# Two more groups' output products by Strassen's seven products, and v of 13 tiles loaded as float by SyncE, in a fused retention and feed-forward kernel on one Trainium2 core

## The chip, the cores and the metric

One core of one Trainium2 chip runs the whole program. Its engines are TensorE (PE; its weight loads are listed as PEld), VectorE (DVE), ScalarE (ACT), GpSimd (POOL) and SyncE (SP), each with its own queue of instructions; they wait for each other by semaphores. The metric is device time in microseconds (us) of one execution. Of the kernel before, three runs gave 205.72, 205.92 and 206.09 us, a median of 205.92 us.

## What is computed

Retention over 4 batches, 8 heads, 768 tokens and 64 columns a head, then a feed-forward network on the 3072 tokens, 512 wide with 2048 hidden columns:

```python
for t in range(S):
    state = gamma[None, :, None, None] * state + np.einsum('bhd,bhe->bhde', k[:, :, t], v[:, :, t])
    y[:, :, t] = scale * np.einsum('bhd,bhde->bhe', q[:, :, t], state)
...
x = np.ascontiguousarray(attn_out.transpose(0, 2, 1, 3)).reshape(B * S, H * D)
...
h = x @ w_in
s = np.sin(alpha * h)
g = h + s * s / (alpha + 1e-09)
return (g @ w_out).astype(np.float32)
```

Inputs and output are float32. The kernel holds operands in bfloat16 and adds up in float32.

## The kernel before, in words

**Tiles, groups, phases.** The 3072 tokens are 24 tiles of 128 (six chunks for each batch). A list P sets their order, and they form ten groups, g = 0 to 9: four tiles, then eight pairs, then four tiles. The recurrence is computed by chunks: for a tile the products of q and k, masked, times v, plus q times the state that the earlier chunks left (`burst` for one tile, `pair` for two). The result is the group's xT, the input of its feed-forward part. Up to the middle of group 1 the order of all work is written out in a list of words; from group 2 on it is set by `phase(g)`.

**A phase.** `phase(g)` computes the hidden layer of group g and, woven into it, the output of group g - 1. For a pair of tiles it has eight slots. A `Slot` takes two of the 16 hidden blocks: 8 matmuls 256 columns wide into a PSUM tile ph (L610), the sine on ScalarE (L613), its square on ScalarE (L618) and, one slot later, h + s²/α on VectorE into gT (`add`, L625). Behind the matmuls of each slot stand those of the output of group g - 1. In some slots `att` puts the attention of a later group in between, and what it leaves to VectorE follows: masks (L404, L407), the state's update (L568, L572) and, in the next two slots, the two halves of xT (`exit0`, `exit1`, L561). `at((g, n), ...)` names such a place by phase and slot; `mixes((g, n), ...)` puts work behind the slot's VectorE work.

**The output in the plain way.** 32 matmuls 512 wide for a pair of tiles (L634, four to a slot), then a copy of each tile from PSUM by VectorE (L644) and its store by SyncE (L647).

**The output by seven products.** For groups in `fast` (before: the pair of group 8 and the two pairs of group 9) the 2x2 blocks of tiles, hidden halves and output columns are multiplied by Strassen's seven products: 56 matmuls 256 wide for a pair (class `Seven`, `mm`, L756). They need sums and differences of gT blocks (`mix_g`, L710, three instructions for two slots' blocks: s, d and x) and of w_out blocks (`mix_w`, L681). The products add up in three PSUM tiles, a, b and c. b is copied to SBUF (`hold`, L765 on ScalarE or L767 on VectorE), and VectorE forms the four output blocks: `cross` (L791, a + b), `rest` (L796, c - b), `main` (L801, a + rest).

**PSUM.** Tag `mm` has four banks, which ph, the plain output and the separate score tiles pb share; `pa` and `two` are tiles of two banks each. The pair's y lies in `two`.

**Loads and turns.** The last 13 tiles of P (`wide`) are read in sets for each batch by `load_seq`: eight transfers for q, k or v, one for each head, issued by GpSimd and converted to bfloat16 on the way (L149). `load_chunk` reads v of earlier tiles (L125). Before a tile's attention its q and k are transposed by a DMA that SyncE issues (`turn`, L297), and its v is multiplied by its decay (`scale_v`, L189) on VectorE or GpSimd. The places of these calls stand at the end of the program, in the tables of `at` and `mixes`.

**Numbers of lines.** All line numbers are those of the kernel before; in the changed kernel L149 is L155, L189 is L197, L297 is L304, L404 and L407 are L411 and L414, L495 is L502, L515 is L522, L561 is L568, L568 is L575, L572 is L579, L610, L613, L618 and L625 are L617, L620, L625 and L632, L644 is L651, L681 is L686, L710 is L717, L756 is L763, L765 is L772, and L791, L796 and L801 are L798, L803 and L808.

Of the kernel before, what the change touches and what calls it, by code (L numbers as in the profile page):

```python
# [38 lines left out]
def kernel(  # L39
# [90 lines left out]

    def load_seq(bt, names="qkv", part=slice(None), between=None):
# [8 lines left out]
        fs = slice(2 * (now[0] - cs[0]), 2 * (now[-1] - cs[0]) + 2)  # L140
        for name, src in (("q", q), ("k", k), ("v", v)):
            if name not in names:
                continue
            for n, (b, m, e) in enumerate(heads):
                if n == 3 and between is not None:
                    scale_v(between, nc.gpsimd)
                r, at = half(b), 2 * m + e
# [1 line left out]
                nc.gpsimd.dma_start(out=o, in_=src[bt, head(b, m, e), now[0] * C:(now[-1] + 1) * C, :].rearrange("(f i) d -> i f d", i=64))  # L149
# [35 lines left out]
    def scale_v(j, eng):  # L185
        t, by = raw["v", j], kg
        if wide(j):
            t, by = t.rearrange("i f p d -> i (f p) d"), kgq
        eng.tensor_mul(t, t, by[:, j % NCH, :, None].to_broadcast([128, H, D]))  # L189

# [473 lines left out]
    w_todo = [(n, i) for n in (4, 3, 1, 7, 6) for i in range(2)]

    def w_homes():
        for _ in range(5):
            yield big.tile([128, 4, NH], BF16, name="w_mix", tag="qkr", bufs=10)
        for pool, tag, n in ((consts, "dec", 2), (big, "qk_seq1", 3)):
            t = pool.tile([128, n, 4, NH], BF16, name="w_mix", tag=tag)  # L670
            for i in range(n):
                yield t[:, i]
    w_home = w_homes()

    def mix_w(eng):

        n, i = w_todo.pop(0)
# [3 lines left out]
        eng.tensor_tensor(w_mix[n, i], w_block(*a, js), w_block(*b, js), op=op)  # L681

# [37 lines left out]
    class Seven:  # L720
# [20 lines left out]
        def right(self, n, j):  # L741
            if n in (5, 2):
                return w_out[:, j + FH * (n == 5), NH * (n == 5):NH * (n == 5) + NH]
            return w_mix[n, j // 4][:, j % 4]

# [303 lines left out]
    load_seq(1, "v")
    load_seq(2, "q")  # L1050
    load_seq(2, "k")
    load_seq(2, "v")
    load_seq(3, "q", slice(0, 2))
    load_seq(3, "k", slice(0, 2))
    for j in P[15:17] + P[18:19]:
        scale_v(j, nc.gpsimd)

# [27 lines left out]
    at((8, 6), B(P[23], None, None, None, None))  # L1085
    for i, spot in ((19, (6, 1)), (20, (6, 5)), (21, (7, 1)), (22, (7, 5)), (23, (8, 0))):
        at(spot, X(P[i]))
    for i, spot in ((19, (6, 2)), (20, (6, 6)), (21, (7, 2)), (22, (7, 6)), (23, (8, 2))):
        at(spot, lambda j=P[i]: scale_v(j, nc.gpsimd))

    def last_loads():
        mix_w(nc.gpsimd)
        nc.gpsimd.tensor_copy(seen, st["qkT", P[17]][:, 0, 0:1])
        load_seq(3, "v")
        mix_w(nc.gpsimd)
        mix_w(nc.gpsimd)
# [50 lines left out]
```

## Time and profile before

| | us |
|---|---|
| median of three runs | 205.92 |
| the profiled execution's own time | 207.02 |
| its span, first to last instruction | 205.2 |
| PE busy | 195.2 |
| DVE busy | 161.5 |
| ACT busy | 151.8 |
| POOL busy | 163.2 |

Times in a profile start at the span's start. In a group's row the busy time and the mean of one instruction in ns stand behind the first bar, the idle time ahead of these instructions and what ended it behind the second. In a timeline the row gives start, busy time, engine, line, operation, and in brackets the idle time ahead of it. The mean granted clock of TensorE was 0.997.

### The profile page before, as it was taken

How to read it: one execution, taken by the hardware profiler on the slowest of the kernel's cores; microseconds unless marked ns; L12 is line 12 of the kernel's file. 1: busy time of each engine (PE TensorE's matmuls, PEld its weight loads, DVE VectorE, ACT ScalarE, POOL GpSimd, SP SyncE). 2: the span in 40 equal slices, each digit the busy share in tenths (PEclk: the TensorE clock that was granted, in tenths of full speed). 3: DMA queues.
4: the chain of work that ended last, by engine and by line, in shares of the span. 5: the costliest groups of instructions: out<-in, count | busy, mean ns of one | idle time of the engine just before them, and what ended most of it. 6: DMA issues, size and time to landing. Idle time of an engine off the chain costs nothing.

```text
span 205.2 us, 6029 instructions
## 1 busy us (share of the span) xinstructions
PE 195.2 (95%) x2426; PEld 131.4 (64%) x2455; DVE 161.5 (79%) x344; ACT 151.8 (74%) x312; POOL 163.2 (80%) x204
## 2 busy tenths in 40 slices
PE   7889999999998999999999999999999999999993
PEld 7444544557765667666666676666766665555983
DVE  5787499877998887887998885995998775577853
ACT  7678888656996877877877959588586869999120
POOL 8998996999999996997399997999193876997000
PEclk9999999999999999999999999999999999999998
DMA  8999999999999999999996796994406101001123
GB/s 133 147 175 192 201 201 176 167 134 106 231 151 188 104 171 194 170 136 150 143 116 117 89 141 117 120 131 104 105 2 107 51 5 51 3 0 51 54 102 102
DMA packets 103580, 24.82 MB, mean 121 GB/s; under 512 B 93392, under 2 KB 101248, under 8 KB 103552
## 3 DMA queue, kind: packets, MB, share of 16 engines
q0 software_dynamic: 80080, 13.38, 92.8%
q1 hardware_dynamic: 23472, 11.06, 26.8%
q8 instruction: 19, 0.31, 0.7%
q14 instruction: 9, 0.07, 0.1%
HBM read 27.30 MB, written 6.29 MB: 164 GB/s over the span
## 4 chain that ended last, share of the span: by engine, by line
PE 83%; DMA 7%; POOL 4%; issue 2%; DVE 2%; ACT 1%; POOLq 0%
PE ph L610 37%; PE po L634 28%; DMA qkT<-qkr 4%; PE a L756 3%; DMA qkr<-in_q_dram 3%; PE ab L756 3%; POOL qkr L125 2%; PE b L756 2%; PE py L373 1%; POOL vr L125 1%; PE c L756 1%; PE pt L291 1%; PE pa L388 1%; PE py L437 1%; POOL w_in L161 1%
## 5 line engine op out<-in xcount | busy, mean ns | idle before, releaser
L625 DVE SCALAR_TENSOR_TENSOR gT<-s,rec_alpha,ph 128x256 bf16<-128x256 f32 (+3 forms) x164 | 79.4, 522 | 25.1 <-ACT s L618 24.6
L610 PE MATMUL ph<-xT,w_in 128*128 128x256 bf16 (+3 forms) x653 | 98.0, 291 | 0.3
L613 ACT ACTIVATE s<-ph,alpha_sb 128x256 f32<-128x256 f32 (+3 forms) x164 | 75.9, 505 | 28.1 <-PE ph L610 26.3
L610 PEld LDWEIGHTS <-w_in 128*128 128x128 bf16 x656 | 63.1, 98 | 29.6 <-DVE s_f L568 0.7
L634 PE MATMUL po<-w_out,gT 128*128 128x512 bf16 x264 | 70.3, 379 | 2.3 <-issue 1.9
L618 ACT ACTIVATE s<-s 128x512 f32<-128x512 f32 (+1 forms) x94 | 58.7, 626 | 2.8
L634 PEld LDWEIGHTS <-gT 128*128 128x128 bf16 x288 | 26.4, 98 | 20.8 <-DVE gT L625 0.5
L710 POOL TENSOR_TENSOR g_mix<-gT 128x512 bf16<-128x512 bf16 (+1 forms) x27 | 25.9, 994 | 7.2 <-DVE gT L625 7.2
L149 POOL DMA_DIRECT2D qk_seq<-in_q_dram x32 | 21.5, 712 | 6.6 <-DMA v_seq<-in_v_dram 6.1
L149 POOL DMA_DIRECT2D qk_seq<-in_k_dram x32 | 21.3, 720 | 1.5 <-DMA qk_seq<-in_q_dram 1.4
L149 POOL DMA_DIRECT2D v_seq<-in_v_dram x24 | 16.8, 743 | 0.0
L681 POOL TENSOR_TENSOR w_mix<-w_out 128x1024 bf16<-128x1024 bf16 x7 | 15.2, 2190 | 0.0
L756 PEld LDWEIGHTS <-g_mix 128*128 128x128 bf16 x128 | 11.9, 98 | 3.6
L644 DVE COPY o_sb<-po 128x512 f32<-128x512 f32 x15 | 10.3, 687 | 2.0 <-PE po L634 1.6
L125 POOL DMA_DIRECT2D vr<-in_v_dram x11 | 10.3, 932 | 1.2 <-DMA w_in<-in_moe_w_in_dram 0.7
L189 POOL TENSOR_TENSOR v_seq<-v_seq,kgq 128x512 bf16<-128x512 bf16 x9 | 9.8, 1097 | 1.4 <-DMA v_seq<-in_v_dram 1.4
L407 DVE TENSOR_TENSOR aTw<-pa,maskq 128x768 bf16<-128x768 f32 x10 | 9.5, 954 | 0.0
L495 DVE TENSOR_TENSOR xT<-py,qg 128x512 bf16<-128x512 f32 x13 | 8.9, 683 | 0.5 <-PE py L453 0.5
L869 PE MATMUL spare<-warm 128*128 128x112 bf16 (+1 forms) x52 | 7.9, 325 | 1.4 <-DVE warm L199 1.2
L391 DVE TENSOR_TENSOR aT<-pa,mask 128x1024 bf16<-128x1024 f32 x7 | 8.5, 1219 | 0.4 <-PE pa L388 0.4
L520 ACT CAST s_q<-s_f 128x256 bf16<-128x256 f32 x13 | 5.1, 393 | 2.7 <-DVE s_f L515 2.7
L165 POOL DMA_DIRECT2D w_out<-in_moe_w_out_dram x8 | 5.8, 727 | 1.2 <-DMA w_in<-in_moe_w_in_dram 0.8
(138 smaller groups left out, 217.7 us busy)
## 6 DMA issues: line engine op xcount, KB each, us to landing
out_dram<-o_sb SPq DMA_DIRECT2D x21, 256.0 KB, 3.9
w_in<-in_moe_w_in_dram POOLq DMA_DIRECT2D x8, 256.0 KB, 8.3
w_out<-in_moe_w_out_dram POOLq DMA_DIRECT2D x8, 256.0 KB, 7.9
vr<-in_v_dram POOLq DMA_DIRECT2D x11, 128.0 KB, 5.3
v_seq<-in_v_dram POOLq DMA_DIRECT2D x16, 80.0 KB, 4.7
qkr<-in_q_dram POOLq DMA_DIRECT2D x7, 128.0 KB, 6.4
qkr<-in_k_dram POOLq DMA_DIRECT2D x7, 128.0 KB, 5.8
qk_seq<-in_q_dram POOLq DMA_DIRECT2D x16, 48.0 KB, 4.4
```

Of the source, the lines that this page charges most:

```text
L125: nc.gpsimd.dma_start(out=t, in_=chunk_of(src, j))
L149: nc.gpsimd.dma_start(out=o, in_=src[bt, head(b, m, e), now[0] * C:(now[-1] + 1) * C, :].rearrange("(f i) d -> i f d", i=64))
L189: eng.tensor_mul(t, t, by[:, j % NCH, :, None].to_broadcast([128, H, D]))
L610: nc.tensor.matmul(self.ph[:, m, :], w_in[:, i, f * 128:(f + 1) * 128], xT[g][:, i, self.lo:self.hi], start=(m == 0 and i == 0), stop=(i = ...
L613: nc.scalar.activation(out=self.s[:, m, :], in_=self.ph[:, m, :], func=ACTF.Sin, scale=alpha_sb[:, f:f + 1])
L618: nc.scalar.activation(out=self.s, in_=self.s, func=ACTF.Square)
L625: nc.vector.scalar_tensor_tensor(gT[self.g][:, f, self.lo:self.hi], self.s[:, m, :], rec_alpha[:, f:f + 1], self.ph[:, m, :], op0=ALU.mult ...
L634: nc.tensor.matmul(po[g, ts], gT[g][:, f, ts * C:(ts + 1) * C], w_out[:, f, :], start=(f == 0), stop=(f == FF - 1))
L644: nc.vector.tensor_copy(o_sb, po[g, ts])
L681: eng.tensor_tensor(w_mix[n, i], w_block(*a, js), w_block(*b, js), op=op)
L710: eng.tensor_tensor(o, i0, i1, op=op)
L756: nc.tensor.matmul(t, self.left(n, j), r, start=k not in self.begun, stop=(j == FH - 1), skip_group_check=True)
```

## The change

1. **Two more groups by seven products.** `fast` goes from (8, 9) to (6, 7, 8, 9), so that the outputs of groups 6 and 7 take seven products each, in phases 7 and 8: five pairs in place of three. `fast_pieces` writes out for each which products stand in which slot, and the PSUM tiles: for group 7 a, b and c in `mm`; for group 6 a in `mm`, b and c one after the other in `two`. `hold` of both goes to ScalarE. `mix_g` for groups 6 and 7 goes to GpSimd, at the places that only group 8 had. `exit1` comes ahead of the slot's `add` in slot 5 of phases 7 to 9.
2. **w_mix** is made early, in phases 2 to 5, in smaller pieces and other homes; two pieces on VectorE, the others on GpSimd.
3. **v of the 13 tiles** comes as float32 by SyncE into a tile vf, which shares its place with gT of groups 0 and 9; `scale_v` reads vf and writes the bfloat16 v. All but P[9]'s of the scales that VectorE had go to GpSimd.
4. **The last q** comes in one set of eight transfers in place of two.
5. **Turns** of P[12], P[17], P[18] and P[19] are issued earlier, and the loads' places move into the phases.
6. The two blocks of a `store_both` go out by one transfer, except in group 8.

The core of the diff:

```diff
-                nc.gpsimd.dma_start(out=o, in_=src[bt, head(b, m, e), now[0] * C:(now[-1] + 1) * C, :].rearrange("(f i) d -> i f d", i=64))
+                o = vf[r, fs, at, :] if name == "v" else tqk[r, fs, "qk".index(name), at, :]
+                (nc.sync if name == "v" else nc.gpsimd).dma_start(out=o, in_=src[bt, head(b, m, e), now[0] * C:(now[-1] + 1) * C, :].rearrange("(f i) d -> i f d", i=64))
...
     def scale_v(j, eng):
         t, by = raw["v", j], kg
+        o = t
         if wide(j):
-            t, by = t.rearrange("i f p d -> i (f p) d"), kgq
-        eng.tensor_mul(t, t, by[:, j % NCH, :, None].to_broadcast([128, H, D]))
+            o, t = (x.rearrange("i f p d -> i (f p) d") for x in (t, raw["vf", j]))
+            by = kgq
+        eng.tensor_mul(o, t, by[:, j % NCH, :, None].to_broadcast([128, H, D]))
...
-    fast = (8, 9)
+    fast = (6, 7, 8, 9)
...
-            if self.g < NG - 1:
+            if self.g == NG - 2:
                 self.store(0, o[:, 0], n)
                 self.store(1, o[:, 1], 1 - n)
                 return
...
+        if g == NG - 3:
+            s = Seven(g, 0, lambda k: psum.tile([128, 2, NH], F32, name=k, tag="mm", bufs=4)[:, slice(0, 2) if k != "c" else 0])
+            parts = [[(4, range(7))], [(4, range(7, FH)), (3, range(6))], [(3, range(6, FH)), (5, range(5))],
+                     [(5, range(5, FH)), (2, range(4))], [(2, range(4, FH)), s.hold], [s.cross, (1, J)], [s.rest, (7, J)],
+                     [(6, J), s.main]]
+            return [s.steps(*p) for p in parts]
+        if g < NG - 3:
+            def between(k):
+                if k == "a":
+                    return psum.tile([128, 2, NH], F32, name=k, tag="mm", bufs=4)
+                return psum.tile([128, 2, 512], F32, name=k, tag="two")[:, 0].rearrange("p (x n) -> p x n", x=2)[:, slice(0, 2) if k == "b" else 0]
+            s = Seven(g, 0, between)
+            parts = [[(4, J)], [(5, J)], [(2, J), s.hold], [(3, J), s.cross], [(7, range(6))], [(7, range(6, FH)), (6, range(4))],
+                     [(6, range(4, FH)), (1, range(3))], [(1, range(3, FH)), s.rest, s.main]]
+            return [s.steps(*p) for p in parts]
...
+            if g - 1 in fast and n == 5:
+                run(more, "exit1")
...
-    for spot in ((7, 0), (7, 2), (7, 6), (7, 7)):
-        mixes(spot, lambda: mix_w(nc.gpsimd))
-    for m in range(0, FH, 2):
-        mixes((8, m + 1), lambda m=m: mix_g(8, m, 2, nc.gpsimd))
...
+    for g in (6, 7, 8):
+        for m in range(0, FH, 2):
+            mixes((g, m + 1), lambda g=g, m=m: mix_g(g, m, 2, nc.gpsimd))
```

What this makes of GpSimd's queue between phases 2 and 4, right behind the k of batch 1 (qk_seq_1194 before, qk_seq_1193 after) and v of P[10] (vr): before, v of batches 1 and 2 stands between the loads of q and k (v_seq_1195 and v_seq_1224; qk_seq_1223 is batch 2's and qk_seq_1249 batch 3's).

```order
L149 DMA qk_seq_1194<-in_k_dram 64x6x64 x8
L125 DMA vr<-in_v_dram 128x8x64
L149 DMA v_seq_1195<-in_v_dram 64x6x64 x8
L149 DMA qk_seq_1223<-in_q_dram 64x10x64 x8
L149 DMA qk_seq_1223<-in_k_dram 64x10x64 x8
L149 DMA v_seq_1224<-in_v_dram 64x10x64 x8
L149 DMA qk_seq_1249<-in_q_dram 64x4x64 x8
L149 DMA qk_seq_1249<-in_k_dram 64x4x64 x8
L189 TENSOR_TENSOR v_seq_1224<-v_seq_1224,kgq 128x512 x3
```

The same place of GpSimd's queue after (qk_seq_1357 is batch 2's, qk_seq_1384 batch 3's; the first scale is that of P[10], the last two are those of P[14] and P[15]).

```order
L125 DMA vr<-in_v_dram 128x8x64
L686 TENSOR_TENSOR w_mix<-w_out 128x512 x2
L197 TENSOR_TENSOR vr<-vr,kg 128x512
L686 TENSOR_TENSOR w_mix<-w_out 128x512 x2
L155 DMA qk_seq_1357<-in_q_dram 64x10x64 x8
L155 DMA qk_seq_1357<-in_k_dram 64x10x64 x2
L197 TENSOR_TENSOR v_seq_1194<-vf,kgq 128x512
L155 DMA qk_seq_1357<-in_k_dram 64x10x64 x6
L197 TENSOR_TENSOR v_seq_1194<-vf,kgq 128x512 x2
L686 TENSOR_TENSOR w_mix<-w_out 128x512 x3
L155 DMA qk_seq_1384<-in_q_dram 64x10x64 x8
L155 DMA qk_seq_1384<-in_k_dram 64x4x64 x8
```

The 16 transfers of v have left this queue; seven small w_mix and four scales, one of them of P[10], stand in it instead.

On VectorE, phase 7 from slot 3 to slot 6, before: the copy of the first output tile, the attention of the pair that follows, and the two halves of xT with an `add` between them.

```order
L644 COPY o_sb<-po 128x512
L625 SCALAR_TENSOR_TENSOR gT<-s,rec_alpha,ph 128x256 x2
L407 TENSOR_TENSOR aTw<-pa,maskq 128x768
L568 TENSOR_TENSOR s_f<-s_f,pa 128x256
L625 SCALAR_TENSOR_TENSOR gT<-s,rec_alpha,ph 128x256 x2
L572 TENSOR_TENSOR s_f<-s_f,pb_3016 128x128
L572 TENSOR_TENSOR s_f<-s_f,pb_3017 128x128
L404 TENSOR_TENSOR aTw<-pb_3016,maskq 128x384
L404 TENSOR_TENSOR aTw<-pb_3017,maskq 128x384
L561 TENSOR_TENSOR xT<-y,qg 128x2x2x128
L625 SCALAR_TENSOR_TENSOR gT<-s,rec_alpha,ph 128x256 x2
L561 TENSOR_TENSOR xT<-y,qg 128x2x2x128
```

The same place on VectorE after: the crossed blocks of group 6 stand where the copy stood, both halves of xT come together, and `rest` and `main` follow two `add`s later.

```order
L798 TENSOR_TENSOR o_sb<-a,b_sb 128x512
L632 SCALAR_TENSOR_TENSOR gT<-s,rec_alpha,ph 128x256 x2
L414 TENSOR_TENSOR aTw<-pa,maskq 128x768
L575 TENSOR_TENSOR s_f<-s_f,pa 128x256
L632 SCALAR_TENSOR_TENSOR gT<-s,rec_alpha,ph 128x256 x2
L579 TENSOR_TENSOR s_f<-s_f,pb_3072 128x128
L579 TENSOR_TENSOR s_f<-s_f,pb_3073 128x128
L411 TENSOR_TENSOR aTw<-pb_3072,maskq 128x384
L411 TENSOR_TENSOR aTw<-pb_3073,maskq 128x384
L568 TENSOR_TENSOR xT<-y,qg 128x2x2x128 x2
L632 SCALAR_TENSOR_TENSOR gT<-s,rec_alpha,ph 128x256 x4
L803 TENSOR_TENSOR t_sb<-c,b_sb 128x512
```

The second half of xT is one `add` earlier in the queue, and the copy of one output tile is replaced by a sum that needs b's copy on ScalarE.

More of the change, by code (lines that the diff above doesn't have):

```diff
@@ L129, in wide, with load_seq @@
         return j >= NCH + 3 and j % NCH > 0
-    def load_seq(bt, names="qkv", part=slice(None), between=None):
+    def load_seq(bt, names="qkv", part=slice(None), between={}, some=slice(None)):
         cs = [c for c in range(NCH) if wide(bt * NCH + c)]
@@ L140, in load_seq @@
         fs = slice(2 * (now[0] - cs[0]), 2 * (now[-1] - cs[0]) + 2)
+        if "v" in names and "vf" not in raw:
+            raw["vf"] = work.tile([128, 16, NP, D], F32, name="vf", tag="gA", bufs=1)
         for name, src in (("q", q), ("k", k), ("v", v)):
@@ L143, in load_seq @@
                 continue
-            for n, (b, m, e) in enumerate(heads):
-                if n == 3 and between is not None:
-                    scale_v(between, nc.gpsimd)
+            if name == "v":
+                vf = raw["vf"][:, 6:16] if bt == 2 else raw["vf"][:, 0:nh]
+                for i, c in enumerate(cs):
+                    raw["vf", bt * NCH + c] = vf[:, 2 * i:2 * i + 2]
+            for n, (b, m, e) in list(enumerate(heads))[some]:
+                if n in between:
+                    between[n]()
                 r, at = half(b), 2 * m + e
-                o = tv[r, fs, at, :] if name == "v" else tqk[r, fs, "qk".index(name), at, :]
-                nc.gpsimd.dma_start(out=o, in_=src[bt, head(b, m, e), now[0] * C:(now[-1] + 1) * C, :].rearrange("(f i) d -> i f d", i=64))
+                o = vf[r, fs, at, :] if name == "v" else tqk[r, fs, "qk".index(name), at, :]
+                (nc.sync if name == "v" else nc.gpsimd).dma_start(out=o, in_=src[bt, head(b, m, e), now[0] * C:(now[-1] + 1) * C, :].rearrange("(f i) d -> i f d", i=64))
         for i, c in enumerate(cs):
@@ L663, with mix_w @@
              6: ((0, 0), (0, 1), ALU.add), 7: ((1, 0), (1, 1), ALU.add)}
[L664 to L677, printed above, removed]
-        a, b, op = W_MIX[n]
-        js = slice(4 * i, 4 * i + 4)
-        w_mix[n, i] = next(w_home)
-        eng.tensor_tensor(w_mix[n, i], w_block(*a, js), w_block(*b, js), op=op)
+    w_todo = {"vr": [(n, j, 2) for n in (7, 6) for j in range(0, FH, 2)] + [(1, 4, 2), (1, 6, 2)],
+              "dec": [(4, 0, 4), (4, 4, 4)], "seq": [(3, 0, 4), (3, 4, 4), (1, 0, 4)]}
+    w_home = {}
+    def mix_w(eng, home):
+        n, i, c = w_todo[home].pop(0)
+        a, b, op = W_MIX[n]
+        if home == "vr":
+            to = big.tile([128, 2, NH], BF16, name="w_mix", tag="vr", bufs=11)
+        else:
+            if home not in w_home:
+                w_home[home] = (consts if home == "dec" else big).tile(
+                    [128, 2 if home == "dec" else 3, 4, NH], BF16, name="w_mix", tag="dec" if home == "dec" else "qk_seq1")
+            to = w_home[home][:, (2 if home == "dec" else 3) - 1 - len(w_todo[home])]
+        eng.tensor_tensor(to, w_block(*a, slice(i, i + c)), w_block(*b, slice(i, i + c)), op=op)
+        for j in range(c):
+            w_mix[n, i + j] = to[:, j]
     def blocks(t, first, *dims):
@@ L743, in right @@
                 return w_out[:, j + FH * (n == 5), NH * (n == 5):NH * (n == 5) + NH]
[L744 removed]
+            return w_mix[n, j]
         def mm(self, n, j, half=None):
@@ L810, in main, with steps @@
                 self.store(1, self.o[:, 1, c], 1, c.start, c.stop)
+        def steps(self, *parts):
+            return [fn for part in parts for fn in ([part] if callable(part) else self.pieces(part))]
         def pieces(self, *parts):
@@ L878, in phase @@
     def phase(g, outs, att, nf=1, on_vector=(), tags={}, early=()):
-        no, done = len(outs), 0
+        plan = outs if outs and isinstance(outs[0], list) else None
+        no, done = 0 if plan else len(outs), 0
         for n in range(FF // nf):
@@ L901, in phase @@
                 rest[0] = fresh
+            for fn in plan[n] if plan else ():
+                fn()
             while done < min(no, no * (n + 1) * nf // FF):
@@ L1044, with scaled @@
         act(word)
-    load_seq(1, "q", between=P[8])
+    def scaled(*js):
+        return lambda: [scale_v(j, nc.gpsimd) for j in js]
+    load_seq(1, "q", between={3: scaled(P[8])})
     load_seq(1, "k")
     load_chunk(P[10], "v")
[L1049 to L1056, printed above, removed]
     where = {}
@@ L1072, in B, with pieces_w @@
         return lambda: burst(old, new, first, beside=beside, second=second)
+    def pieces_w(n, home):
+        return lambda: [mix_w(nc.gpsimd, home) for _ in range(n)]
     for n in range(9, 17):
@@ L1077 @@
         at(where[n], B(P[n - 1], new, first, P[17] if n == 16 else None, e3 if n == 15 else None))
-        at(where[n] if n < 16 else (5, 5), X(P[n + 2]))
+        if n != 10:
+            at({15: (4, 6), 16: (4, 5)}.get(n, where[n]), X(P[n + 2]))
     for i, spot in ((16, (6, 4)), (18, (7, 4)), (20, (8, 1))):
@@ L1091, in last_loads @@
     def last_loads():
[L1092 to L1096, printed above, removed]
+        load_seq(3, "k", slice(2, None))
+        scale_v(P[16], nc.gpsimd)
         scale_v(P[17], nc.gpsimd)
-        load_seq(3, "qk", slice(2, None))
     at((5, 5), last_loads)
-    for i, spot in ((9, (2, 3)), (10, (3, 0)), (11, (3, 3)), (12, (3, 7)), (13, (4, 3)), (14, (4, 6))):
+    for i, spot in ((9, (2, 3)),):
@@ L1102, with loads @@
         at(spot, lambda j=P[i]: scale_v(j, nc.vector))
     at((2, 0), later_mask)
+    def loads():
+        load_seq(1, "v")
+        turn(P[12])
+        pieces_w(2, "vr")()
+        scale_v(P[10], nc.gpsimd)
+        pieces_w(2, "vr")()
+        load_seq(2, "q")
+        load_seq(2, "k", between={2: scaled(P[11])})
+        scale_v(P[12], nc.gpsimd)
+        scale_v(P[13], nc.gpsimd)
+        pieces_w(3, "vr")()
+        load_seq(3, "q")
+        load_seq(3, "k", slice(0, 2))
+    at((2, 2), loads)
@@ L1113 @@
+    for spot in ((4, 2), (4, 3)):
+        mixes(spot, lambda: mix_w(nc.vector, "vr"))
+    for spot, fn in (((3, 6), scaled(P[14], P[15])), ((3, 6), pieces_w(1, "dec")),
+                     ((3, 6), pieces_w(1, "dec")), ((4, 5), pieces_w(3, "seq")), ((4, 5), pieces_w(1, "vr"))):
+        mixes(spot, fn)
+    for g in (6, 7, 8):
+        for m in range(0, FH, 2):
+            mixes((g, m + 1), lambda g=g, m=m: mix_g(g, m, 2, nc.gpsimd))
     for m in range(FH):
```

12 lines of the change are left out of this document (6 added, 6 removed).

## The prediction, made before the changed kernel was run

> **What bounds the kernel now.** I read the page's busy times, then the chain of waits (start, length, what), then the stretch from 140 to 170 us in windows of 10 us (window, sum, busy time and instructions of PE, PEld, DVE, ACT and POOL, clock, DMA share).
>
> ```profile
> PE 195.2 (95%) x2426; PEld 131.4 (64%) x2455; DVE 161.5 (79%) x344; ACT 151.8 (74%) x312; POOL 163.2 (80%) x204
> ```
> ```profile
> 54.89 7.37 DMA qkT<-qkr
> 64.73 0.86 PE po L634 x4
> 196.82 0.87 PE c L756 x8
> ```
> ```profile
> 140.00:150.00 10.00, 9.95 (x173) 6.91 (x173) 7.84 (x18) 7.26 (x16) 5.46 (x5) 1.00 0.38 85
> 150.00:160.00 10.00, 9.79 (x143) 6.91 (x142) 7.74 (x16) 7.56 (x17) 6.48 (x5) 1.00 0.32 56
> 160.00:170.00 10.00, 9.64 (x135) 6.39 (x135) 7.84 (x17) 7.33 (x18) 7.91 (x9) 1.00 0.08 29
> ```
>
> TensorE is busy for 9.6 to 9.95 of each 10 us, at a granted clock of 1.00, in the phases that the change rewrites. Time can go only where TensorE's own work gets less, and any wait put before it shows in full. VectorE, ScalarE and GpSimd have 2 to 4.5 us of each 10 us left. The largest single wait of the chain, the transposition at 54.89, lies ahead of everything that the change moves; I leave it as it is.
>
> **Part 1a: the matmuls saved.** A plain output costs a pair eight steps like the one at 64.73, 8 x 0.86 = 6.88 us. Seven products cost seven steps like the one at 196.82, 7 x 0.87 = 6.09 us. That is 0.79 us a pair, 1.58 us for two pairs. Weight loads do not spoil it: the eight matmuls of c took 0.87 us with theirs beside them.
>
> **Part 1b: what phase 7 gives back.** The prices of the new steps stand in the view of the tiles b_sb and t_sb (count, least, median, most in ns):
>
> ```profile
> L765 ACT COPY b_sb<-b x2: 585/585/585, 195.8 to 196.6; 128x512 f32<-128x512 f32 x2
> L791 DVE TENSOR_TENSOR o_sb<-ab,b_sb x1: 692/692/692, 183.5 to 183.5; 128x512 f32<-128x512 f32 x1
> L796 DVE TENSOR_TENSOR t_sb<-c,b_sb x3: 681/684/691, 185.4 to 200.4; 128x512 f32<-128x512 f32 x3
> ```
>
> Two copies from PSUM of 0.69 us become a copy on ScalarE and three sums on VectorE: 0.69 us more for VectorE and 0.59 for ScalarE in each phase. There is room on average; the question is the place. These are ScalarE, VectorE and TensorE in phase 7 now:
>
> ```profile
> 143.04 0.63 ACT L618 ACTIVATE s<-s 128x512 f32<-128x512 f32 x1
> 143.91 0.84 ACT L613 ACTIVATE s<-ph,alpha_sb 128x256 f32<-128x256 f32 x2 [0.24 <-PE ph L610]
> ```
> ```profile
> 138.50 0.87 DVE L625 SCALAR_TENSOR_TENSOR gT<-s,rec_alpha,ph 128x256 bf16<-128x256 f32 x2
> ...
> 144.77 0.69 DVE L644 COPY o_sb<-po 128x512 f32<-128x512 f32 x1 [0.20 <-PE po L634]
> 145.44 0.87 DVE L625 SCALAR_TENSOR_TENSOR gT<-s,rec_alpha,ph 128x256 bf16<-128x256 f32 x2
> 146.32 0.96 DVE L407 TENSOR_TENSOR aTw<-pa,maskq 128x768 bf16<-128x768 f32 x1
> ...
> 149.63 0.68 DVE L561 TENSOR_TENSOR xT<-y,qg 128x512 bf16<-128x512 f32 x1
> 150.32 0.87 DVE L625 SCALAR_TENSOR_TENSOR gT<-s,rec_alpha,ph 128x256 bf16<-128x256 f32 x2
> 151.11 0.68 DVE L561 TENSOR_TENSOR xT<-y,qg 128x512 bf16<-128x512 f32 x1
> ```
> ```profile
> 139.36 1.04 PE L610 MATMUL ph<-xT,w_in 128*128 128x256 bf16 x8
> ...
> 142.84 1.04 PE L610 MATMUL ph<-xT,w_in 128*128 128x256 bf16 x8
> 143.71 1.03 PE L634 MATMUL po<-w_out,gT 128*128 128x512 bf16 x4
> 144.57 1.04 PE L610 MATMUL ph<-xT,w_in 128*128 128x256 bf16 x8
> ...
> 147.71 1.04 PE L610 MATMUL ph<-xT,w_in 128*128 128x256 bf16 x8
> ```
>
> By the starts a slot's ph takes 0.87 us (142.84 to 143.71) and its four plain output matmuls 0.86. `hold` follows the square that ends at 143.67, so it ends at 144.25 and the next sine starts 0.35 us late. `add` follows at about 145.8 in place of 145.44, and from there VectorE has no gap up to the second half of xT. That half now comes ahead of its `add`: without delay it would start at 149.63 + 0.68 = 150.31, with it at 150.68, and end at 151.36. For it waits c, which gets the two banks of `two` that y holds. TensorE comes there earlier than before: the slot that begins at 147.71 begins some 0.2 us sooner (six products, 0.65 us, where four wide matmuls of 0.86 stood), so 147.5 + 0.87 + 0.65 + 0.87 + 0.44 = 150.3. The wait is 151.36 - 150.3, about 1.0 us, the new last wait of the phase. It takes the place of any smaller one before it (score tiles and ph of the banks a has taken). Bounds: 0 if VectorE runs 1.0 us ahead of this, 1.3 if the row lags by another 0.3. I take 0.8, since VectorE's 0.2 us of hand-over ahead of the copy at 144.77 takes up part of a late row, and 0.1 for the first products, which want the `add` of group 6's last blocks (it ends at 139.37). Phase 7: -0.79 + 0.9 = +0.1 us.
>
> The Trainium skill speaks against this step: "Trainium Kernel Development and Optimization", Best Practices, says that tiling on TensorE speeds up compute but not PSUM evacuation. The rows of b_sb and t_sb agree, three sums and a copy for two copies; by the rule alone, evacuation would close both phases and the change would give 205.9 us, where the sum by rows below gives 205.6.
>
> **Part 1c: phase 8.** With a, b and c in `mm`, ph has two of the four banks for most of the phase. From the start of a ph to the end of its `add` go 0.87 + 0.84 + 0.63 + 0.87 and two hand-overs of some 0.1 to 0.25: 3.3 to 3.6 us. Two slots of 0.87 + 0.76 (seven products) are 3.3 us long. So most slots of this phase wait 0 to 0.3 us; over six slots I put 0.4 (bounds 0 and 1.5). `hold` adds 0.1. Phase 8: -0.79 + 0.5 = -0.3 us. Group 8's pair, in phase 9, stays as it was.
>
> **Parts 2 to 5: GpSimd and the loads.** GpSimd's groups and their idle time:
>
> ```profile
> L710 POOL TENSOR_TENSOR g_mix<-gT 128x512 bf16<-128x512 bf16 (+1 forms) x27 | 25.9, 994 | 7.2 <-DVE gT L625 7.2
> L149 POOL DMA_DIRECT2D qk_seq<-in_q_dram x32 | 21.5, 712 | 6.6 <-DMA v_seq<-in_v_dram 6.1 <-DMA vr<-in_v_dram 0.3
> L149 POOL DMA_DIRECT2D qk_seq<-in_k_dram x32 | 21.3, 720 | 1.5 <-DMA qk_seq<-in_q_dram 1.4
> L149 POOL DMA_DIRECT2D v_seq<-in_v_dram x24 | 16.8, 743 | 0.0
> L681 POOL TENSOR_TENSOR w_mix<-w_out 128x1024 bf16<-128x1024 bf16 x7 | 15.2, 2190 | 0.0
> L189 POOL TENSOR_TENSOR v_seq<-v_seq,kgq 128x512 bf16<-128x512 bf16 x9 | 9.8, 1097 | 1.4 <-DMA v_seq<-in_v_dram 1.4
> ```
>
> The 24 issues of v go (16.8 us), and eight of q (8 x 0.71 = 5.7 us); what they cost SyncE lies in its idle time. In their place come five scales of 1.10 us, four more parts of g_mix for each of two groups (8 x 2.9 = 23 us) and about as much w_mix as before. GpSimd so has more work than before, and it has dates to keep (GpSimd, then TensorE):
>
> ```profile
> 67.28 0.91 POOL L125 DMA_DIRECT2D vr<-in_v_dram  x1 [0.17 <-issue]
> 79.24 2.13 POOL L149 DMA_DIRECT2D qk_seq<-in_q_dram  x3 [2.04 <-DMA v_seq<-in_v_dram]
> 107.88 1.06 POOL L189 TENSOR_TENSOR v_seq<-v_seq,kgq 128x512 bf16<-128x512 bf16 x1
> ```
> ```profile
> 85.99 0.30 PE L421 MATMUL pa<-v_seq,qk_seq 64*64 64x64 bf16 x16
> 109.46 0.30 PE L421 MATMUL pa<-v_seq,qk_seq 64*64 64x64 bf16 x16
> ```
>
> From 68.19 on, where v of P[10] is issued, stand seven halves of w_mix (7 x 1.10), four scales (4 x 1.10) and 32 issues (32 x 0.72), 35.1 us; the scale of P[10] waits about 2 us for v to land. P[14] is scaled at 68.2 + 35.1 + 2 + 1.1 = 106.4 us; TensorE reads it at 109.46: 3.1 us to spare. P[11], after 4 halves, 2 scales and 10 issues, is ready at 84.2 and read at 85.99. I cost all this at nothing. What covers it is those 3.1 us, and they hold only if GpSimd no longer waits for earlier transfers before it issues the next: before, it lost 6.6 + 1.5 = 8.1 us so, 6.1 of them for v, which is no longer in its queue. On SyncE, turns and stores now stand behind v's transfers. The later sets of v wait for the scales of P[14] and P[15] to free their part of vf, and behind them stand stores only until phase 6; if these scales are late, the stores and with them the tiles o_sb are late too.
>
> VectorE loses five scales and one w_mix, and one copy in a phase where it has time over; TensorE is full there (9.6 to 9.95), so I count a gain of 0.1 (bounds 0 and 0.3). The last part: one transfer for two stores saves SyncE's time only, nothing.
>
> **The sum.** -1.58 saved, +0.9 given back in phase 7, +0.5 in phase 8, and -0.1 for VectorE's smaller load: -0.3 us. That makes a span of 204.9 for the 205.2 of the profiled execution. That execution took 207.02 in all, 1.8 more than its span; the median of 205.92 is 0.7 above the span, and the forecast 0.7 above 204.9: 205.6 us. A measurement of this kernel tells from no change about 0.2%, 0.41 us.
>
> **The rivals.**
> - A, the forecast: the saving is paid back by waits for PSUM behind VectorE, 205.6 us, itself between 205.2 and 206.1. For it: the rows of phase 7, in which VectorE has no gap for 6 us. Chance 0.45.
> - B, the saving is kept: the waits for c and ph fall in time that TensorE loses anyway, or the chain is 1 us shorter than I made it. Then 205.92 - 1.58 + 0.1 = 204.4 us. For it: the windows leave VectorE 2.2 us in ten; against it, they are not at this place. Chance 0.28.
> - C, GpSimd comes late. If half of the 8.1 us of waits stay, 4.05 us, P[14]'s scale comes 4.05 - 3.1 = 1 us after TensorE wants it; and in phase 7 each part of g_mix delayed holds up the product that reads it, where GpSimd can have the last s sums at 139.37 + 0.99 = 140.4 at best and the last b products read them at 139.36 + 0.87 + 6 x 0.11 = 140.9, for another 0.6 us. 205.6 + 1.6 = 207.2 us. It decides from 3.1 us of waits before the scale of P[14]. For it: 32 narrow transfers still stand in a row, now beside v's float transfers with the same rows; in the row at 79.24 one wait alone is 2.04 us. Against it: 24 fewer transfers in that queue. Chance 0.27.
>
> The Trainium skill ("DMA: Bandwidth & Descriptors", Issuing engines are not separate DMA queues) says that DMAs started by different engines run on the same 16 DMA engines, and that spreading the issuing saves only the sequencer's time. By that rule C's waits stay, for the bytes do not get fewer; the trace of before cannot show it, since there v's loads had one issuer.
>
> That the seven products do not come is excluded, since the order lists them.
>
> **How the numbers follow.** Range: 204.4 (B) to 207.1 (most of C; 207.2 is its middle), leaving out B's lower part and C's worst. Faster by over 0.2% (below 205.5): B's 0.28 and 0.16 of A, 0.44. Within: 0.27 of A and 0.03 of the others, 0.30. Slower (above 206.33): 0.24 of C and 0.02 of A, 0.26. Cases of both signs hold the chance; A's own range is 205.2 to 206.1.
>
> **What would show it.** In the changed kernel's timeline: seven products of 0.87 us in phases 7 and 8; TensorE idle for some 1 us ahead of c in phase 7, ended by VectorE's xT; idle of 0.1 to 0.3 us before ph in phase 8, ended by gT; GpSimd's scale of P[14] done by 107 and no wait of TensorE for v. Without the idle time ahead of c, B is right; with idle time of TensorE ended by v_seq, g_mix or qkT, C. I am wrong altogether if the difference lies before 60 us or in phase 9.

## The result, and the profile after

The changed kernel took 213.82 us (median of four runs, 211.49 to 215.54), the kernel before beside it 205.82; the ratio is 1.0295 with a 95% interval of 1.0263 to 1.0327. The forecast was 205.6 us, the range went up to 207.1. The ratio leaves out the two longest executions (215.54 and 215.52 us), the first of which is the one of the profile shown (span 213.8), while the two medians take in all and lie 8.0 us, or 3.9%, apart.

The busy times on the page of the changed kernel:

```profile
PE 199.5 (93%) x2503; PEld 136.9 (64%) x2503; DVE 158.9 (74%) x340; ACT 152.8 (71%) x314; POOL 174.5 (82%) x206
```

TensorE's share fell from 95 to 93%. Who waited for whom, first TensorE, then GpSimd (us in all, times, longest):

```profile
PE y L444 <- POOL v_seq L197: 6.3, 1, 6.3
PE pa L402 <- DMA qkT<-qk_seq: 1.6, 1, 1.6
```
```profile
POOL v_seq L197 <- DMA out_dram<-o_sb: 8.6, 1, 8.6
POOL qk_seq L155 <- DMA qk_seq<-in_q_dram: 4.9, 5, 1.5
```

One wait of 6.3 us is most of the loss: TensorE waits for GpSimd's scale of a v, and GpSimd had waited 8.6 us for a transfer that SyncE issued. The profile names a store there, but the instruction reads vf, and the last v transfer was issued right ahead of that store, at 130.01 us, and landed 6.8 us later. TensorE and GpSimd around it, in order of time:

```profile
131.42 0.34 PE L444 MATMUL y<-aTw,v_seq 64*64 64x128 bf16 x16
138.06 0.54 PE L444 MATMUL y<-aTw,v_seq 64*64 64x128 bf16 x16 [6.29 <-POOL v_seq L197]
```
```profile
127.22 1.13 POOL L197 TENSOR_TENSOR v_seq<-vf,kgq 128x512 bf16<-128x512 f32 x1
136.97 1.04 POOL L197 TENSOR_TENSOR v_seq<-vf,kgq 128x512 bf16<-128x512 f32 x1 [8.62 <-DMA out_dram<-o_sb]
```

SyncE's queue (SPq) from 95 to 132 us tells why the v was late. Behind it stand what one issue of v costs (least, median and most in ns) and one of SyncE's waits in this stretch:

```profile
95.06 1.23 SPq L304 DMA_TRANSPOSE qkT<-qk_seq  x1
96.35 5.53 SPq L155 DMA_DIRECT2D vf<-in_v_dram  x8
101.98 0.54 SPq L654 DMA_DIRECT2D out_dram<-o_sb  x1
102.62 2.05 SPq L304 DMA_TRANSPOSE qkT<-qk_seq  x1
104.76 0.65 SPq L654 DMA_DIRECT2D out_dram<-o_sb  x1
105.51 10.59 SPq L304 DMA_TRANSPOSE qkT<-qk_seq  x4
116.14 6.47 SPq L155 DMA_DIRECT2D vf<-in_v_dram  x8
122.73 0.55 SPq L654 DMA_DIRECT2D out_dram<-o_sb  x1
123.38 8.16 SPq L155 DMA_DIRECT2D vf<-in_v_dram  x8
```
```profile
L155 SPq DMA_DIRECT2D vf<-in_v_dram x32: 601/624/1539, 71.2 to 130.0; - x32
```
```profile
SPq L304 <- DMA qk_seq<-in_k_dram: 2.7, 1, 2.7
```

SyncE has next to no free time from 95 to 132 us. Four turns take 10.6 us, 2.7 of which are a wait for batch 3's k from GpSimd's queue; the two sets of v behind them take 6.5 and 8.2 us, and between them lies a store. So the last v is issued by 131.5, lands at about 137, and is scaled at 138. The turn of P[15] stands behind the set that began at 96.35; issued at 102.62, it lands at 109.99, and TensorE waits 1.6 us for it until 110.03.

Counting the sines on ScalarE (164 in each kernel, in the same order) tells where the time went. The table gives the start of the first sine of each phase, before, and how much later it began in a profiled execution of the changed kernel and of some runs described below:

| phase | 2 | 3 | 4 | 5 | 6 | 7 | 8 | 9 | last sine |
|---|---|---|---|---|---|---|---|---|---|
| before, us | 60.26 | 76.15 | 91.82 | 107.40 | 123.72 | 138.70 | 154.00 | 170.79 | 189.48 |
| changed | +0.17 | -1.09 | -1.09 | -1.00 | +0.75 | +9.06 | +9.11 | +8.61 | +8.62 |
| e1_again (the same kernel) | -0.32 | -0.18 | -0.18 | -0.09 | +1.26 | +7.64 | +7.69 | +7.19 | +7.19 |
| e2_three_pairs | -0.47 | -1.73 | -1.73 | -1.64 | -0.71 | +6.84 | +6.84 | +6.84 | +6.84 |
| e4_turns_back | +1.13 | +0.00 | +0.00 | +0.09 | +2.58 | +4.24 | +4.28 | +3.78 | +3.78 |
| e8_turn19 | -0.40 | -1.51 | -1.51 | -1.42 | -0.38 | +0.03 | +0.29 | -0.20 | -0.20 |
| e9_turns18_19 | -0.45 | -1.53 | -1.26 | +0.38 | +4.00 | +4.31 | +4.35 | +3.85 | +3.86 |
| e11_three_pairs_8 | +0.40 | -0.75 | -0.75 | -0.66 | -0.58 | -0.00 | -0.00 | -0.00 | -0.00 |
| e12_before_turns | -0.18 | -1.27 | -1.27 | -1.27 | -1.08 | -1.08 | -1.08 | -1.08 | -1.08 |

The 1.1 to 1.3 us that some rows gain from phase 2 to 3 are a wait at 62 us in the profile of before:

```profile
PE pa L388 <- DMA qkT<-qkr: 1.1, 1, 1.1
```

The changed kernel did not have it in its first profile and had it in its second (e1_again, 1.3 us), so it is no gain of the change. Then, in the changed kernel, come 1.75 us in phase 5 and 8.3 in phase 6, +0.05 in phase 7, -0.50 in phase 8.

The 8.3 us are more than the 6.3 waited. The windows of the changed kernel around the wait show the rest (window, its length, busy time and instructions of PE, PEld, DVE, ACT and POOL, clock, DMA share, GB/s):

```profile
131.00:134.00 3.00, 0.77 (x64) 0.63 (x60) 2.72 (x6) 1.45 (x3) 0.00 (x0) 1.00 1.45 177
134.00:137.00 3.00, 0.00 (x0) 0.00 (x0) 0.00 (x0) 0.00 (x0) 0.03 (x1) 0.73 1.29 304
137.00:138.00 1.00, 0.00 (x0) 0.00 (x0) 0.00 (x0) 0.00 (x0) 1.00 (x2) 0.50 1.52 105
138.00:142.00 4.00, 3.94 (x58) 2.44 (x59) 2.02 (x5) 0.00 (x0) 4.00 (x6) 0.50 0.16 37
142.00:146.00 4.00, 4.00 (x29) 2.70 (x27) 1.66 (x4) 2.94 (x6) 3.21 (x4) 0.97 0.00 0
```

During the wait the granted clock fell to 0.50 and stayed there for the first four us of work: some 2 us more. The Trainium skill ("TensorE: Matmul & The Clock Gate", Part 1: The HAM clock gate) says that TensorE's clock goes to half after an idle window of about 3.4 us and comes back after about as long a busy one; these rows agree. Their means put the fall some 3.6 us into the wait and the return some 4.2 us after the matmuls began again, an estimate from 0.73 in the window from 134 us and 0.97 in the one from 142. A shorter wait, which does not fit the rule, stands in the last section.

### The profile page after: what moved, and what is told of

Read it like the earlier page. It is cut to its first block, busy times and chain, and to the rows that moved or that the text cites. A ratio compares the mean times of both kernels' runs of the same rounds, so it can differ in the third digit from the quotient of the medians.

```text
span 213.8 us, 6205 instructions
## 1 busy us (share of the span) xinstructions
PE 199.5 (93%) x2503; PEld 136.9 (64%) x2503; DVE 158.9 (74%) x340; ACT 152.8 (71%) x314; POOL 174.5 (82%) x206
## 4 chain that ended last, share of the span: by engine, by line
PE 74%; DMA 9%; POOL 6%; DVE 6%; ACT 3%; issue 1%; SPq 0%; POOLq 0%; ACTq 0%
PE ph L617 33%; PE po L641 22%; PE a L763 5%; DMA w_out<-in_moe_w_out_dram 3%; DMA qkT<-qk_seq 3%; POOL qkr L125 2%; PE ab L763 2%; PE b L763 2%; DVE gT L632 2%; POOL vr L125 2%; PE c L763 2%; DMA out_dram<-o_sb 2%; ACT s L620 1%; PE py L380 1%; DVE aTw L414 1%; PE pt L298 1%
## 5 line engine op out<-in xcount | busy, mean ns | idle before, releaser
L641 PE MATMUL po<-w_out,gT 128*128 128x512 bf16 x224 | 59.1, 384 | 0.1
L717 POOL TENSOR_TENSOR g_mix<-gT 128x512 bf16<-128x512 bf16 (+1 forms) x51 | 49.0, 997 | 3.5 <-DVE gT L632 3.1
L641 PEld LDWEIGHTS <-gT 128*128 128x128 bf16 x224 | 20.7, 98 | 16.9 <-issue 0.5
L763 PEld LDWEIGHTS <-g_mix 128*128 128x128 bf16 x208 | 19.4, 98 | 5.4 <-DVE xT L568 0.6
L197 POOL TENSOR_TENSOR v_seq<-vf,kgq 128x512 bf16<-128x512 f32 x13 | 13.6, 1052 | 9.2 <-DMA out_dram<-o_sb 8.6
L686 POOL TENSOR_TENSOR w_mix<-w_out 128x512 bf16<-128x512 bf16 (+1 forms) x13 | 19.5, 1528 | 0.0
L155 POOL DMA_DIRECT2D qk_seq<-in_q_dram x24 | 16.9, 745 | 1.0 <-DMA vr<-in_v_dram 1.0
L763 PEld LDWEIGHTS <-gT 128*128 128x128 bf16 x88 | 7.9, 98 | 2.2 <-DVE gT L632 0.3
L651 DVE COPY o_sb<-po 128x512 f32<-128x512 f32 x11 | 7.6, 690 | 1.7 <-PE po L641 1.3
L763 PE MATMUL a<-w_mix,gT 128*128 128x256 bf16 (+1 forms) x72 | 8.7, 261 | 0.0
L763 PE MATMUL b<-w_out,g_mix 128*128 128x256 bf16 x64 | 8.3, 273 | 0.0
```

The costliest lines, as they stand in the source:

```text
L155: (nc.sync if name == "v" else nc.gpsimd).dma_start(out=o, in_=src[bt, head(b, m, e), now[0] * C:(now[-1] + 1) * C, :].rearrange("(f i) d ...
L197: eng.tensor_mul(o, t, by[:, j % NCH, :, None].to_broadcast([128, H, D]))
L641: nc.tensor.matmul(po[g, ts], gT[g][:, f, ts * C:(ts + 1) * C], w_out[:, f, :], start=(f == 0), stop=(f == FF - 1))
L686: eng.tensor_tensor(to, w_block(*a, slice(i, i + c)), w_block(*b, slice(i, i + c)), op=op)
L717: eng.tensor_tensor(o, i0, i1, op=op)
L763: nc.tensor.matmul(t, self.left(n, j), r, start=k not in self.begun, stop=(j == FH - 1), skip_group_check=True)
```

## The experiments

The theories after the result. **Q**: the harm comes from SyncE's queue, in which v stands behind turns that wait for GpSimd's k, and turns behind v. **D**: the 16 DMA engines are full, and any order would be as slow. **S**: the seven products cost it. Ratios are to the kernel before on the same chip, with their 95% intervals. The first four ran together, then three, three and two.

**e1_again.** No edit.

> The changed kernel once more, for a second profile. Theory Q (SyncE's queue: the last v stands behind turns that wait for GpSimd's k): TensorE stalls again at one place, about 131 us, ended by GpSimd's scale of P[17], for 3 to 7 us, with SyncE's last v issued behind four turns. Theory D (the 16 DMA engines are full there) expects the same stall. Rival S (the seven products cost it): no such stall, the loss spread over phases 7 and 8. The wait at 62 us may come back (1.3 us) if it was only an early or late landing. About 212 us.

Measured: 1.0342 (1.0258 to 1.0426). The same place, a wait of 4.6 us, and the loss in phases 5 and 6 as in the table; the median of 215.15 us lies above the 212 expected. The wait at 62 us was back. The loss is not spread over phases 7 and 8, as S would have it.

**e2_three_pairs.**

```diff
-    fast = (6, 7, 8, 9)
+    fast = (8, 9)
...
-    for g in (6, 7, 8):
+    for g in (8,):
         for m in range(0, FH, 2):
```

> The changed kernel with only the three old pairs by seven products; groups 6 and 7 plain. Q and D: the stall at 131 us stays whole, and the time is that of the changed kernel plus 0.4 to 0.5 us, which the two new pairs bring net by the count of sines in the two traces. Rival S: it falls to 206 us.

Measured: 1.0415 (1.0342 to 1.0488), with a wait for the same scale of 5.6 us. In the table it neither loses nor gains in phases 7 and 8 (+6.84 throughout), where the five-pair form gains 0.45 (+7.64 to +7.19). The loss is whole without the two new pairs: it comes from what the change did to the loads, the turns and GpSimd's queue. S is out.

**e3_v2_early.**

```diff
-    at((3, 6), lambda: load_seq(2, "v", slice(0, 2)))
-    at((4, 6), lambda: load_seq(2, "v", slice(2, None)))
+    at((3, 1), lambda: load_seq(2, "v"))
```

> The changed kernel with v of batch 2 in one set at (3, 1), where SyncE stood idle for 11 us, in place of two sets at (3, 6) and (4, 6). Same bytes, eight issues fewer, and nothing of batch 2's v between the turns. Q: the last v is issued some 6.5 us sooner (116 to 124 us), lands by 130, and the stall at 131 goes; the turn of P[15] comes sooner too, and the 1.6 us at 110 go: 203 to 204.5 us. D: the transfers collide with batch 2's q and k instead, the turns land later by as much, and the time stays within 1.5 us of the changed kernel's.

Measured: 1.0487 (1.0422 to 1.0552), no faster than the changed kernel (1.0342 in e1_again; the two intervals just touch). TensorE's wait, SyncE's queue, and the landing of the turns issued from 100 to 105 us (median, us):

```profile
PE pa L402 <- DMA qkT<-qk_seq: 8.4, 1, 8.4
```
```profile
84.09 15.20 SPq L155 DMA_DIRECT2D vf<-in_v_dram  x8
99.39 1.17 SPq L654 DMA_DIRECT2D out_dram<-o_sb  x1
100.92 2.90 SPq L304 DMA_TRANSPOSE qkT<-qk_seq  x1
```
```profile
qkT<-qk_seq SPq DMA_TRANSPOSE x2, 9.3
```

The miss is plain: I had taken SyncE's idle time there for free. Beside batch 2's q and k the eight issues took 15.2 us in place of the 5 to 8 of other sets, and the turn of P[14] behind them came at 100.92 in place of 95.06. TensorE waited 8.4 us for it. The order is the smaller part of this. The turn landed at 110.42 in place of 98.20, 12.2 us later: 6.4 of these are its landing (9.5 us from the issue for 3.1), 3.7 are batch 2's k, which the turn reads and which landed at 98.4 for 94.7, and some 2 are left for the queue. So D is right for this stretch: the transfers slow each other, and the issues of v themselves hold SyncE longer (1.9 us each).

**e4_turns_back.**

```diff
-            at({15: (4, 6), 16: (4, 5)}.get(n, where[n]), X(P[n + 2]))
+            at(where[n] if n < 16 else (5, 5), X(P[n + 2]))
...
-    for i, spot in ((19, (4, 6)), (20, (6, 5)), (21, (7, 1)), (22, (7, 5)), (23, (8, 0))):
+    for i, spot in ((19, (6, 1)), (20, (6, 5)), (21, (7, 1)), (22, (7, 5)), (23, (8, 0))):
```

> The changed kernel with the turns of P[17], P[18] and P[19] at their old places, (5, 1), (5, 5) and (6, 1). Not a byte less; SyncE's rest of batch 2's v no longer stands behind turns that wait for batch 3's k. Q: the last v is issued by 125 us and lands by 131, the stall at 131 shrinks from 6 us to under 1.5, and a wait of up to 2 us for the turn of P[17] may come at 118: 205 to 208 us. D: the last v lands no sooner than 135, and the time stays above 210.

Measured: 1.0133 (1.0072 to 1.0194), a median of 209.27 us, above Q's 205 to 208 and below D's 210. SyncE's queue and TensorE's waits:

```profile
104.67 3.50 SPq L304 DMA_TRANSPOSE qkT<-qk_seq  x1
108.22 6.85 SPq L155 DMA_DIRECT2D vf<-in_v_dram  x8
115.18 1.26 SPq L654 DMA_DIRECT2D out_dram<-o_sb  x1
117.24 1.28 SPq L304 DMA_TRANSPOSE qkT<-qk_seq  x1
118.62 6.82 SPq L155 DMA_DIRECT2D vf<-in_v_dram  x8
```
```profile
PE pa L402 <- DMA qkT<-qk_seq: 1.9, 2, 1.0
PE pb L402 <- DMA qkT<-qk_seq: 1.6, 2, 1.3
```

The last v is issued by 125.4 and lands at 130.4, where D had it no sooner than 135, and TensorE no longer waits for it at all; the same bytes moved, six us sooner. Four waits for turns of up to 1.3 us remain. The order of one queue was thus worth about three fifths of the loss (from 3.4 to 1.3%).

**e5_w_mix_behind, e6_order, e7_order_split.** e5 is e4 with this besides:

```diff
-        pieces_w(3, "vr")()
         load_seq(3, "q")
         load_seq(3, "k", slice(0, 2))
...
-    for spot, fn in (((3, 6), scaled(P[14], P[15])), ((3, 6), pieces_w(1, "dec")),
+    for spot, fn in (((3, 6), scaled(P[14], P[15])), ((3, 6), pieces_w(3, "vr")), ((3, 6), pieces_w(1, "dec")),
```

> The run with the three turns at their old places, and besides GpSimd's three small w_mix (3.4 us) behind batch 3's q and k in place of ahead of them. Nothing left out. Theory Q (what SyncE's queue waits for is k by GpSimd): k of batch 3 lands 3 us sooner (111 for 114 us), the turn of P[17] no longer holds TensorE (1.4 us at 120 before), the other three waits for turns stay, 207 to 208 us. Theory D (the DMA engines are full and set the landing): k lands within 1 us of before, and the time stays at 209.

e6 has this too, but the turn of P[15] at (3, 6), those of P[17] and P[18] where the change put them, and that of P[19] at (5, 3):

> The changed kernel with its turns of P[16], P[17] and P[18] where the change put them, that of P[15] ahead of batch 2's first v, that of P[19] behind the last v, and w_mix behind batch 3's q and k. Q: the waits for turns of P[15] (1.0 to 1.7 us) and of P[17] go, the last v is issued from about 119 us and lands by 131, so the stall at 131 stays under 1.5 us: 205.5 to 207.5 us. D: the last v lands at 135 as in the changed kernel, above 210 us.

e7 is e6 with the last v in two sets, at (5, 2) and (5, 3):

> As the run before, and the last v in two sets: eight small transfers with P[17]'s part alone, the turn of P[19], then the rest. Eight issues of 0.62 us more for SyncE, the same bytes. Q: P[17]'s v lands by 127, no stall at 131; the rest lands by 134, in time for P[18]: 0 to 1 us better than the run before. D: no better than it.

Measured: e5 1.0177 (1.0118 to 1.0236), e6 1.0193 (1.0129 to 1.0256), e7 1.0191 (1.0135 to 1.0247); none better than e4 by its interval, and Q's times (207 to 208 us for e5, 205.5 to 207.5 for e6) missed: the medians are 209.9 to 210.5, beside 206.75 of the kernel before there. But the wait moved each time. In e5 P[17]'s turn is issued at 113.78 in place of 117.24 and its wait is gone, as Q said, and one long wait of TensorE is left, for the turn of P[19], which stands behind the last v:

```profile
PE pb L402 <- DMA qkT<-qk_seq: 3.8, 1, 3.8
```

In e6 the last v landed at 129.3, not at the 135 of D, and it is GpSimd that comes late, with scales and, in phase 7, with g_mix:

```profile
PE pa L428 <- POOL v_seq L197: 2.0, 2, 1.1
PE b L763 <- POOL g_mix L717: 0.9, 1, 0.9
```
```profile
109.97 2.05 POOL L197 TENSOR_TENSOR v_seq<-vf,kgq 128x512 bf16<-128x512 f32 x2 [4.88 <-DMA vf<-in_v_dram]
```

This row of e6 is the scale of P[14] and P[15]. It waits for batch 2's first v and starts at 109.97 in place of 104.77 in e5. The nine w_mix behind it, which e5 has too, the next scales and the first g_mix all start 5.2 us later than in e5. P[15]'s turn, now ahead of that v on SyncE, held it up by 1.6 us; P[14]'s turn, ahead of both, was 1.7 us later already, and the rest went in issuing and landing.

e7 has the same two waits (2.6 and 0.9 us): bringing the last v in two sets gained nothing.

**e8_turn19, e9_turns18_19, e10_k_first.** e8 is e5 with P[19]'s turn at (5, 1):

> The run with w_mix behind batch 3's q and k, and besides P[19]'s turn at (5, 1), ahead of the last v on SyncE, in place of (6, 1) behind it. Theory Q: the 4.0 us that TensorE waited at 134 for this turn go; the last v and P[18]'s turn come 1.3 us later, which may cost up to 1 us at 130: 205.3 to 207 us. Theory D (the DMA engines are the limit, and the order only moves who waits): another transfer comes late instead, the last v or P[18]'s turn by 3 us or more, above 208 us.

e9 is e8 with P[18]'s turn at (4, 5):

> As the run before, and P[18]'s turn at (4, 5), ahead of the rest of batch 2's v. Q: P[18] in time, the last v 2 us later than in the run before, so 1 to 2 us of waiting for P[17]'s scale or turn: 205.5 to 208 us. D: above 208 us.

e10 is e8 with the rest of batch 3's k ahead of the w_mix:

> As the run with P[19]'s turn at (5, 1), and the rest of batch 3's k 15 us sooner on GpSimd, ahead of nine w_mix, so that no narrow loads run beside the last v and P[18]'s turn (122 to 132 us). Q: no change of more than 1 us, unless the rest of batch 2's v comes late. D: the last v lands 2 us or more sooner, but the rest of batch 2's v and P[17]'s turn land later, beside these loads: a wait of 1 to 3 us at 120.

Measured: e8 1.0062 (1.0031 to 1.0093), e9 1.0218 (1.0166 to 1.0269), e10 1.0128 (1.0071 to 1.0185). In e8, for turns, only this is left of TensorE's waits (it waits for no v):

```profile
PE pa L402 <- DMA qkT<-qk_seq: 0.6, 2, 0.3
PE pb L402 <- DMA qkT<-qk_seq: 0.3, 1, 0.3
```

The e5 wait of 3.8 us is gone by one turn moved ahead of eight transfers of v, as Q said, and nothing else came late by 3 us. In e9 one turn more ahead of batch 2's last v costs it back: P[17]'s turn behind that v is issued at 117.44 in place of 114.39 (1.8 us of it for the added turn, the rest from before the edit's place), TensorE waits 1.9 us for it, and with the clock that falls after this wait phase 5 loses 3.6 us, where e8 loses 1.0. Another 1.5 us of e9, at 101.8 us, are a wait for a turn that stands ahead of the edit, so they are not its work. In e10, D's expectation came true in its second half: P[17]'s turn was issued as early as in e8 (114.22 for 114.39), but beside the narrow loads it took 4.7 us to land, not 3.3, and TensorE waited 1.9 us for it.

```profile
PE pb L402 <- DMA qkT<-qk_seq: 1.9, 1, 1.9
```

**e11_three_pairs_8.** e8 with the edit of e2.

> The run with P[19]'s turn at (5, 1), with three pairs by seven products in place of five. If the two new pairs bring 0.45 us net, as the sines of the changed kernel and of its three-pair form say, this run's sines of phases 7 and 8 lose nothing against before, where the five-pair form gains 0.23 us from sine 112 to the end (+0.03 to -0.20), and its time is 0.2 to 0.5 us above the five-pair form's: 207.2 to 207.6 us. If the seven products cost more than they bring there, it is faster than the five-pair form.

Measured: 1.0083 (1.0051 to 1.0116), a median of 207.28 us beside 207.02 of e8. The table has it: unchanged in phases 7 and 8, where e8 goes from +0.03 to -0.20. The intervals overlap; the sines carry the verdict, that two more pairs bring 0.2 us (here) to 0.45 us (e2) net.

**e12_before_turns.** The kernel before, with the turns of P[17], P[18] and P[19] at the change's places, the reverse of e4's edit.

> The kernel before with only the turns of P[17], P[18] and P[19] at the change's earlier places. SyncE then waits at (4, 6) for batch 3's k as in the changed kernel, but has only stores behind it. Theory Q (the harm is v standing behind these turns): within 0.4 us of the kernel before. A rival, that the early turns themselves do the harm by standing in the DMA engines beside narrow loads or by holding the qkT tiles: 1 us or more slower, with TensorE waiting for another turn.

Measured: 1.0005 (0.9988 to 1.0021). SyncE's queue of this run:

```profile
98.90 12.85 SPq L297 DMA_TRANSPOSE qkT<-qk_seq  x4
111.84 11.08 SPq L647 DMA_DIRECT2D out_dram<-o_sb  x3
```

SyncE is held by four turns for 12.9 us, longer than in the changed kernel, and it costs nothing: behind them stand stores. Early turns do no harm by themselves; v behind them does. That is the pair of runs, e4 and e12, that settles the cause of the stall at 131 us.

No run beat the kernel before. What keeps e8 0.6% above it lies by the table in phase 5 (1.0 us), phase 6 (0.4) and phase 7 (0.3). Three waits of 0.3 us for turns are part of it; the rest was not taken apart, and may be D's share.

## Why the prediction was wrong

**The step that failed** is the costing of the loads: "what they cost SyncE lies in its idle time", and "I cost all this at nothing". I added up GpSimd's queue to a tenth of a us and never SyncE's. With the median of 0.62 us that the trace of after has for one issue of v, 32 issues are 20 us; they took 26, and a set of eight in the crowded stretch 6.5 to 8.2. The idle time of SyncE in the trace of before was waiting time:

```profile
SPq L647 <- DVE o_sb L644: 65.0, 12, 8.0
SPq L297 <- DMA qk_seq<-in_k_dram: 16.6, 5, 6.0
```

The queue runs in order, and what was put behind its waits waits too. I named the stores as what stands behind a late vf, and missed that the vf itself stands behind turns which wait for GpSimd. TensorE's 6.3 us wait, with the lowered clock 8.3 us, and the 1.6 us at P[15]'s turn are this step. With the three turns moved behind batch 2's v (e4) the 6.3 us were gone, and with only stores behind the same turns (e12) they cost nothing.

**What held.** The seven products, in the main: phase 7 was put at +0.1 us and measured +0.05, phase 8 at -0.3 and measured -0.50, in the changed kernel and in e1. Within phase 7 the wait for c came where it was expected, ended by VectorE's xT; in e1_again:

```profile
158.85 0.50 PE L763 MATMUL c<-w_mix,g_mix 128*128 128x256 bf16 x3 [0.30 <-DVE xT L568]
```

It is 0.3 us of idle time, not 0.8; the phase gave back 0.84 us all the same. The starts of the matmuls in the trace of after show most of it: the 56 of phase 7 took 6.88 us in place of 7 x 0.87, with 0.46 us more than usual ahead of the first of c, 0.17 among the first eight, where the prediction put 0.1, and 0.11 at one later place. In phase 8 the prediction put 0.4 us of waits ahead of ph, and one of 0.1 us came. (Its own terms for a slot add up to 3.4 to 3.7 us, not 3.3 to 3.6.) The rule of the Trainium skill ("Trainium Kernel Development and Optimization", Best Practices) that tiling on TensorE speeds up compute but not PSUM evacuation held for phase 7 (+0.05 us) and not for phase 8 (-0.50). By e2, the two new pairs bring 0.45 us of the 1.58 us of matmul time saved.

**GpSimd's dates.** P[14] was scaled by 108.46 + 2.05 / 2 = 109.5 us, not 106.4, because 4.9 us of waits for earlier transfers stayed:

```profile
108.46 2.05 POOL L197 TENSOR_TENSOR v_seq<-vf,kgq 128x512 bf16<-128x512 f32 x2
```

TensorE read it at 110.23, after the wait of 1.57 us for P[15]'s turn. Without that wait it would have come at 108.66, 0.8 us before the scale was done, so the late turn hid a late scale.

**Rival C** had the right sign and the wrong place: it let GpSimd be late with P[14] at 109 us and priced the stall at 1.6 us. It was P[17] at 131, through SyncE. By the signs that the prediction named, idle time of TensorE ended by v_seq or qkT, the result is C's; its threshold of 3.1 us of waits was passed, with 4.9, but cost TensorE nothing of its own. The sentence beside it, by the Trainium skill ("DMA: Bandwidth & Descriptors", Issuing engines are not separate DMA queues), that another issuer saves only the sequencer's time, is right on the bytes, as e3 shows; but for the stall at 131 us the sequencer's time and order were the larger part, as e4 and e12 show.

**The vf tile.** The prediction let the later sets of v wait for the scales of P[14] and P[15]. These were done by 110.5 us, and the set that reuses their place began at 123.38: the tile held nothing up.

**The range** ended at 207.1. It was built from cases in which one wait is late by some us; none had a full queue with two kinds of transfers that wait for each other.

## What to carry to other kernels

A queue's idle time in a trace is not free time: for an in-order queue, list what each instruction waits for and what it will hold up, and make the same sum of issue times for the queue that receives work as for the one that is relieved. Where transfers of two kinds share one issuer, put the one that is needed first and whose inputs are ready ahead, and look at the next deadline behind it. A wait of TensorE costs more than its length when the clock falls during or after it.
